# The end of an output projection: wo as the stationary operand, four columns on 128 partitions, and a store from contiguous partitions

## Chip, cores and metric

The kernel runs on one core of one Trainium2 chip. The metric is the device time of one execution in microseconds (us). Kernels that are compared were run in turn on the same chip. The profile's own span (first to last instruction) is usually about 1.8 us shorter than that time. The granted clock is the share of TensorE's full clock that the profile records. HBM is the memory that holds the caches and the result, SBUF the on-chip memory that the loads fill, PSUM the one in which products are summed.

## The reference, cut to what matters

```python
def reference(A_x, A_k_cache, A_v_cache, A_wq, A_wo, B_x, B_w1, B_b1, B_w2, B_b2):
    x = A_x                                    # 1 x 1 x 512
    xn = _layernorm(x, axis=-1)
    # 32 query heads, 8 key/value heads, 65536 keys, head size 128, then o (4096) @ wo (4096 x 512)
    return x + _A_ref(xn, A_k_cache, A_v_cache, A_wq, A_wo) + _B_ref(xn, B_w1, B_b1, B_w2, B_b2)
```

All tensors are bf16. One token attends to 65536 cached keys, so nearly all the work is reading the caches: 268 MB. The result is one row of 512 values, 1 KB.

## The kernel before

The kernel streams both caches, keeps the softmax statistics of each chunk, and combines them at the end. The last loads are the 4 MB of `wo`, in pieces: `wo0` (16 rows of 128 partitions), `wo1` (8 rows), `wo2` (4 rows), and for the last group of heads `wl0` (three heads) and `wl1` (one). What follows is the end, where the change lies. `oX_bf` holds the attention outputs of the first seven groups, `oT_all` those of the last, `f_rows` the sum of everything else as four fp32 rows on partitions 0, 32, 64 and 96 (other partitions are not selected by `row_sel`).

```python
    def fin_mm(kt, lhsT, rhs, reads, first, last, publish):
        sch.op(PE, lambda: pe.matmul(pR[32 * kt:32 * kt + 1, 0:128], lhsT=lhsT, rhs=rhs, start=first, stop=last),
               reads=reads, writes=[f"pss{R}"], publish=publish)

    R0 = WP[0][1] * HPG
    # ... wo0: 16 products of 512 columns into pss1, then f_rows = pss1 + f_rows on VectorE ...
    for i, (g0, n) in enumerate(WP):
        if i == 0:
            continue
        for r in range(g0 * HPG, (g0 + n) * HPG):
            for kt in range(KT):
                fin_mm(kt, oX_bf[:, r:r + 1], wo_sb[:, r, kt * 128:(kt + 1) * 128], ["oX", f"wo{i}"], r == R0, False,
                       r == (g0 + n) * HPG - 1 and kt == KT - 1)
    for kt in range(KT):
        fin_mm(kt, row_sel[:, :], f_rows[:, kt * 128:(kt + 1) * 128], ["f_rows", "row_sel"], False, False, kt == KT - 1)
    for h in range(HPG):
        for kt in range(KT):
            fin_mm(kt, oT_all[:, GE * HPG + h:GE * HPG + h + 1], wl_sb[:, h, kt * 128:(kt + 1) * 128],
                   ["oL", f"wl{0 if h < WH[0] else 1}"], False, h == HPG - 1, h == HPG - 1 and kt == KT - 1)
    NR = 32 * (KT - 1) + 1
    sch.op(DVE, lambda: dve.tensor_copy(out=fin_bf[0:NR, :], in_=pR[0:NR, 0:128]),
           reads=[f"pss{R}"], writes=["fin"])
    ev_out = sch.dma(
        SP,
        lambda: sp.dma_start(out=out[0, 0].rearrange("(kt p) -> kt p", p=128), in_=fin_bf[0:NR:32, :]),
        sem_out, reads=["fin"], writes=["out_dram"],
    )
    sch.wait_ev(SP, ev_out)
```

So the stationary operand (`lhsT`) is one column of attention output, `wo` streams past it 128 columns at a time, and the result is four rows of 128 values on four partitions. The whole kernel:

## Time and profile before

| | before |
|---|---|
| time, median of 6 runs | 658.36 us (658.16 to 658.62) |
| span of the profile | 656.4 us |
| read from HBM | 280.5 MB, 427 GB/s |
| granted TensorE clock, 652 to 653.5 us | 0.50 |
| start of the store's issue to the end of the span | 2.0 us |

Four lines of the page: the span, the busy tenths of the DMA engines in 40 slices, the traffic, and the shares of the chain that ended last.

```profile
span 656.4 us, 27873 instructions
...
DMA  9999999999999999999999999999999999999997
...
HBM read 280.50 MB, written 0.00 MB: 427 GB/s over the span
...
DMA 69%; PE 29%; issue 2%; SPq 0%; DVE 0%
...
```

The DMA engines are at nine tenths in all slices but the last, so the kernel runs at the speed of its loads until about 653 us. The tail after the last load is the only place where this change can cost or gain. The timeline of that tail has the columns start, duration, engine, line, operation, output<-inputs, sizes and count; in brackets stands how long the engine was idle before and what released it. PE is the product, PEld the load of its stationary operand.

```profile
...
start us, us, engine line op out<-in xcount [idle before <-releaser]
...
651.19 1.02 PE L808 MATMUL pss<-kv,oX_bf 128*1 128x128 bf16 x32 [0.21 <-DMA kv<-in_A_wo_dram]
...
652.48 0.59 PE L808 MATMUL pss<-kv,oX_bf 128*1 128x128 bf16 x16 [0.26 <-DMA kv<-in_A_wo_dram]
...
652.86 0.64 PE L808 MATMUL pss<-f_rows,row_sel 128*1 128x128 f32 x8
653.46 0.41 PEld L808 LDWEIGHTS pss<-kv,oT_all 128*1 128x1 bf16 x16 [0.47 <-DMA kv<-in_A_wo_dram]
653.46 0.55 PE L808 MATMUL pss<-kv,oT_all 128*1 128x128 bf16 x16
654.06 0.29 DVE L833 CAST fin_bf<-pss 97x128 bf16<-97x128 f32 x1 [2.33 <-PE pss L808]
654.38 0.63 SPq L837 DMA_DIRECT2D out_dram<-fin_bf  x1
```

Read it in steps. `wo1` lands and releases 32 products at 651.19; `wo2` releases 16 at 652.48. The four fp32 products of `f_rows` appear as eight passes from 652.86, and they end inside the wait for `wl`: the loads of the last 16 products are released by the transfer at 653.46. Those take 0.55 us, the VectorE copy 0.29 us, the issue of the store 0.63 us. After that the SyncE queue only waits for the store to land:

```profile
...
SPq L842 <- DMA out_dram<-fin_bf: 1.0, 1, 1.0
...
```

The windows of the same stretch, with busy us and count per engine, then the granted clock, the DMA share and GB/s:

```profile
...
core 0: us, PE busy (x) PEld busy (x) DVE busy (x) ACT busy (x) POOL busy (x), PEclk, DMA share, GB/s
...
652.40:653.50 1.10, 1.02 (x28) 0.56 (x32) 0.00 (x0) 0.00 (x0) 0.00 (x0) 0.50 0.32 110
653.50:655.50 2.00, 0.51 (x16) 0.25 (x16) 0.29 (x1) 0.00 (x0) 0.00 (x0) 0.97 0.00 0
...
```

### The profile page before, as it was taken

How to read it: one execution, taken by the hardware profiler on the slowest of the kernel's cores; microseconds unless marked ns; L12 is line 12 of the kernel's file. 1: busy time of each engine (PE TensorE's matmuls, PEld its weight loads, DVE VectorE, ACT ScalarE, POOL GpSimd, SP SyncE). 2: the span in 40 equal slices, each digit the busy share in tenths (PEclk: the TensorE clock that was granted, in tenths of full speed). 3: DMA queues.
4: the chain of work that ended last, by engine and by line, in shares of the span. 5: the costliest groups of instructions: out<-in, count | busy, mean ns of one | idle time of the engine just before them, and what ended most of it. 6: DMA issues, size and time to landing. Idle time of an engine off the chain costs nothing.

```text
span 656.4 us, 27873 instructions
## 1 busy us (share of the span) xinstructions
PE 536.7 (82%) x12634; PEld 507.4 (77%) x12634; DVE 276.3 (42%) x576; ACT 245.0 (37%) x454; POOL 2.9 (0%) x27
## 2 busy tenths in 40 slices
PE   2398699979789697878969788896978979797897
PEld 0187698969788696878959687895968879686886
DVE  3254162614435171452616245261633516153353
ACT  0144161613525162352605335161543516144251
POOL 0000000000000000000000000000000000000000
PEclk9688595967869596785959669595976959687695
DMA  9999999999999999999999999999999999999997
GB/s 369 431 445 417 438 423 439 435 427 459 403 439 439 421 445 423 435 431 433 445 415 447 415 447 421 427 461 401 457 413 453 423 423 435 427 459 406 433 429 302
DMA packets 8773, 280.64 MB, mean 428 GB/s; under 512 B 1082, under 2 KB 1596, under 8 KB 1724
## 3 DMA queue, kind: packets, MB, share of 16 engines
q1 hardware_dynamic: 8616, 280.50, 99.3%
q8 instruction: 7, 0.11, 0.1%
q10 hardware_dynamic: 148, 0.01, 0.0%
q14 instruction: 2, 0.02, 0.0%
HBM read 280.50 MB, written 0.00 MB: 427 GB/s over the span
## 4 chain that ended last, share of the span: by engine, by line
DMA 69%; PE 29%; issue 2%; SPq 0%; DVE 0%
DMA kv<-in_A_k_cache_dram 65%; PE pst L591 24%; DMA kv<-in_A_wo_dram 4%; PE pss L611 3%; PE pO L682 1%; PE pss L808 0%; PE pA L638 0%; PE pA L649 0%; SPq L479 0%; DVE pmax L619 0%; PE pA L698 0%; SPq L471 0%; SPq L468 0%; SPq L464 0%; DVE gmax L640 0%
## 5 line engine op out<-in xcount | busy, mean ns | idle before, releaser
L601 ACT ACTIVATE kt_ring<-pst 128x1024 bf16<-128x1024 bf16 x192 | 195.6, 1027 | 311.4 <-PE pst L591 310.0
L591 PE MATMUL pst<-ident_bf,kv 128*128 128x128 bf16 x4096 | 280.8, 234 | 34.8 <-DMA kv<-in_A_k_cache_dram 34.7
L591 PEld LDWEIGHTS pst<-ident_bf,kv 128*128 128x128 bf16 x4096 | 262.5, 106 | 43.2 <-DMA kv<-in_A_k_cache_dram 36.4
L599 DVE COPY kt_ring<-pst 128x1024 bf16<-128x1024 bf16 x320 | 210.6, 687 | 118.7 <-PE pst L591 116.6
L682 PE MATMUL pO<-P_bf,kv 128*128 128x4 bf16 x4096 | 115.1, 166 | 40.8 <-DMA kv<-in_A_v_cache_dram 34.9
L682 PEld LDWEIGHTS pO<-P_bf,kv 128*128 128x128 bf16 x4096 | 113.6, 104 | 42.2 <-DMA kv<-in_A_v_cache_dram 36.0
L611 PE MATMUL pss<-q_cur,kt_ring 128*128 128x4 bf16 x4096 | 111.9, 164 | 2.6 <-issue 2.6
L611 PEld LDWEIGHTS pss<-q_cur,kt_ring 128*128 128x128 bf16 x4096 | 109.3, 96 | 2.8 <-issue 2.8
L660 ACT ACTIVATE P_bf<-pss,negm 128x128 bf16<-128x128 f32 x128 | 50.9, 547 | 67.7 <-DVE negm L652 67.7
L691 DVE COPY o_all<-pO 128x4 f32 (+1 forms) x32 | 5.2, 162 | 124.0 <-PE pO L682 123.2
L619 DVE TENSOR_REDUCE pmax<-pss 128x4 f32<-128x512 f32 x32 | 22.1, 691 | 66.5 <-PE pss L611 66.5
L660 ACT ACTIVATION_READ_ACCUMULATOR P_bf<-pss,negm 128x1 f32 x128 | 35.3, 276 | 0.0
L649 PEld LDWEIGHTS pA<-diag,ones_f 4*128 4x128 f32 x64 | 12.6, 245 | 18.2 <-DVE diag L642 16.5
L638 PE MATMUL pA<-ident_f,pmax 128*4 128x128 f32 x64 | 14.3, 312 | 12.5 <-DVE pmax L619 12.5
L649 PE MATMUL pA<-diag,ones_f 4*128 4x4 f32 x64 | 15.4, 309 | 10.0 <-DVE diag L642 10.0
L638 PEld LDWEIGHTS pA<-ident_f,pmax 128*4 128x4 f32 x64 | 2.9, 84 | 15.7 <-DVE pmax L619 14.0
L640 DVE TENSOR_REDUCE gmax<-pA 4x1 f32<-4x128 f32 x32 | 8.8, 274 | 9.5 <-PE pA L638 9.5
L674 DVE COPY sums_all<-sums 128x8 f32 (+1 forms) x16 | 2.7, 172 | 23.4 <-ACT P_bf L660 23.4
L698 PE MATMUL pA<-sums_all,ones_f 128*128 128x128 f32 x32 | 12.4, 491 | 0.0
L652 DVE TENSOR_SCALAR negm<-pA 128x4 f32<-128x4 f32 x32 | 5.1, 160 | 10.8 <-PE pA L649 10.8
L698 PEld LDWEIGHTS pA<-sums_all,ones_f 128*128 128x128 f32 x32 | 8.1, 312 | 0.0
L642 DVE TENSOR_SCALAR diag<-ident_f,gmax 4x4 f32<-4x4 f32 x32 | 7.0, 217 | 1.1
(82 smaller groups left out, 49.4 us busy)
## 6 DMA issues: line engine op xcount, KB each, us to landing
kv<-in_A_k_cache_dram SPq DMA_DIRECT2D x32, 4096.0 KB, 27.7
kv<-in_A_v_cache_dram SPq DMA_DIRECT2D x4, 4096.0 KB, 24.7
kv<-in_A_wq_dram SPq DMA_DIRECT2D x1, 4096.0 KB, 12.2
kv<-in_B_w_dram SPq DMA_DIRECT2D x2, 1792.0 KB, 18.0
kv<-in_A_wo_dram SPq DMA_DIRECT2D x1, 2048.0 KB, 23.5
kv<-in_A_wo_dram SPq DMA_DIRECT2D x1, 1024.0 KB, 25.7
kv<-in_A_wo_dram SPq DMA_DIRECT2D x1, 512.0 KB, 26.5
kv<-in_A_wo_dram SPq DMA_DIRECT2D x1, 384.0 KB, 16.9
```

The costliest lines, as they stand in the source:

```text
L591: lambda tb=tb, at=at, b=b, tt=s * TPB + t: pe.transpose(pst[tb][:, at * 128:(at + 1) * 128], slot[b][:, tt, :], ident_bf[:, :]),
L599: e, fn = DVE, lambda tb=tb, dst=dst: dve.tensor_copy(out=dst, in_=pst[tb][:, :])
L601: e, fn = ACT, lambda tb=tb, dst=dst: act.activation(out=dst, in_=pst[tb][:, :], func=ACTF.Copy)
L611: lambda k=k, kb=kb, at=at, t=t: pe.matmul(pss[k][:, at:at + HPG], lhsT=kt_ring[:, kb * BCOL + t * 128:kb * BCOL + (t + 1) * 128], rhs=q_c ...
L619: lambda k=k: dve.tensor_reduce(out=pmax[:, :], in_=pss[k][:, 0:CW].rearrange("p (t j) -> p j t", j=HPG), axis=AX.X, op=ALU.max),
L638: sch.op(PE, lambda: pe.matmul(pA[0:HPG, PA_ST:PA_ST + 128], lhsT=pmax[:, 0:HPG], rhs=ident_f[:, :], start=True, stop=True), reads=["pmax" ...
L640: sch.op(DVE, lambda: dve.tensor_reduce(out=gmax4[:, :], in_=pA[0:HPG, PA_ST:PA_ST + 128], axis=AX.X, op=ALU.max), reads=["pA"], writes=[" ...
L642: sch.op(DVE, lambda: dve.tensor_scalar(out=diag4[:, :], in0=ident_f[0:HPG, 0:HPG], scalar1=gmax4[0:HPG, 0:1], scalar2=None, op0=ALU.mult) ...
L649: sch.op(PE, lambda: pe.matmul(pA[:, PA_SB:PA_SB + HPG], lhsT=ones_f[0:HPG, 0:128], rhs=diag4[0:HPG, 0:HPG], start=True, stop=True), reads ...
L660: lambda k=k, at=at, j=j, src=src: act.activation(out=P_v[k][:, :, j], in_=src[:, :, j], func=ACTF.Exp, bias=negm[:, at:at + 1], scale=1.0 ...
L682: lambda k=k, t=t: pe.matmul(pO[:, 0:HPG], lhsT=vslot[:, k * TPD + t, :], rhs=P_v[k][:, t, :], start=t == 0, stop=t == TPD - 1),
L698: sch.op(PE, lambda: pe.matmul(pA[:, PA_SUM:PA_SUM + NC], lhsT=ones_f[:, :], rhs=sums_all[:, :], start=True, stop=True), reads=["ones_f", ...
```

## The change

The idea is to turn the operands round. `wo` becomes the stationary operand (128 columns, taken at a step of four), the attention output streams one column, and the result stands as four columns on 128 partitions: partition p holds outputs 4p to 4p+3. The copy out of PSUM is then 128x4 in place of 97x128, and the store takes 8 contiguous bytes from each of 128 contiguous partitions in place of 256 bytes from each of four.

```diff
-    fin_bf = sb("fin_bf", [128, 128], BF)
+    fin_bf = sb("fin_bf", [128, KT], BF)
 ...
-        sch.op(PE, lambda: pe.matmul(pR[32 * kt:32 * kt + 1, 0:128], lhsT=lhsT, rhs=rhs, start=first, stop=last),
+        sch.op(PE, lambda: pe.matmul(pR[:, kt:kt + 1], lhsT=lhsT, rhs=rhs, start=first, stop=last),
 ...
-                fin_mm(kt, oX_bf[:, r:r + 1], wo_sb[:, r, kt * 128:(kt + 1) * 128], ["oX", f"wo{i}"], r == R0, False,
+                fin_mm(kt, wo_sb[:, r, kt:D:KT], oX_bf[:, r:r + 1], ["oX", f"wo{i}"], r == R0 and kt == 0, False,
 ...
-        fin_mm(kt, row_sel[:, :], f_rows[:, kt * 128:(kt + 1) * 128], ["f_rows", "row_sel"], False, False, kt == KT - 1)
+        fin_mm(kt, f_rows[:, kt:D:KT], row_sel[:, :], ["f_rows", "row_sel"], False, False, kt == KT - 1)
 ...
-            fin_mm(kt, oT_all[:, GE * HPG + h:GE * HPG + h + 1], wl_sb[:, h, kt * 128:(kt + 1) * 128],
+            fin_mm(kt, wl_sb[:, h, kt:D:KT], oT_all[:, GE * HPG + h:GE * HPG + h + 1],
 ...
-    sch.op(DVE, lambda: dve.tensor_copy(out=fin_bf[0:NR, :], in_=pR[0:NR, 0:128]),
+    sch.op(DVE, lambda: dve.tensor_copy(out=fin_bf[:, :], in_=pR[:, 0:KT]), reads=[f"pss{R}"], writes=["fin"])
 ...
-        lambda: sp.dma_start(out=out[0, 0].rearrange("(kt p) -> kt p", p=128), in_=fin_bf[0:NR:32, :]),
+        lambda: sp.dma_start(out=out[0, 0].rearrange("(p kt) -> p kt", kt=KT), in_=fin_bf[:, :]),
```

The code writes the products into the four columns as one accumulation group now: only the first of them has the start flag, and only the last the stop flag.

More of the change, by code (lines that the diff above doesn't have):

```diff
@@ L823, in bass_parallel_sum__gqa_block_cached__dense_activation_gelu__decode_kernel @@
             for kt in range(KT):
-                fin_mm(kt, oX_bf[:, r:r + 1], wo_sb[:, r, kt * 128:(kt + 1) * 128], ["oX", f"wo{i}"], r == R0, False,
+                fin_mm(kt, wo_sb[:, r, kt:D:KT], oX_bf[:, r:r + 1], ["oX", f"wo{i}"], r == R0 and kt == 0, False,
                        r == (g0 + n) * HPG - 1 and kt == KT - 1)
     for kt in range(KT):
-        fin_mm(kt, row_sel[:, :], f_rows[:, kt * 128:(kt + 1) * 128], ["f_rows", "row_sel"], False, False, kt == KT - 1)
+        fin_mm(kt, f_rows[:, kt:D:KT], row_sel[:, :], ["f_rows", "row_sel"], False, False, kt == KT - 1)
     for h in range(HPG):
         for kt in range(KT):
-            fin_mm(kt, oT_all[:, GE * HPG + h:GE * HPG + h + 1], wl_sb[:, h, kt * 128:(kt + 1) * 128],
-                   ["oL", f"wl{0 if h < WH[0] else 1}"], False, h == HPG - 1, h == HPG - 1 and kt == KT - 1)
-    NR = 32 * (KT - 1) + 1
-    sch.op(DVE, lambda: dve.tensor_copy(out=fin_bf[0:NR, :], in_=pR[0:NR, 0:128]),
-           reads=[f"pss{R}"], writes=["fin"])
+            fin_mm(kt, wl_sb[:, h, kt:D:KT], oT_all[:, GE * HPG + h:GE * HPG + h + 1],
+                   ["oL", f"wl{0 if h < WH[0] else 1}"], False, h == HPG - 1 and kt == KT - 1, h == HPG - 1 and kt == KT - 1)
+    sch.op(DVE, lambda: dve.tensor_copy(out=fin_bf[:, :], in_=pR[:, 0:KT]), reads=[f"pss{R}"], writes=["fin"])
     ev_out = sch.dma(
         SP,
-        lambda: sp.dma_start(out=out[0, 0].rearrange("(kt p) -> kt p", p=128), in_=fin_bf[0:NR:32, :]),
+        lambda: sp.dma_start(out=out[0, 0].rearrange("(p kt) -> p kt", kt=KT), in_=fin_bf[:, :]),
         sem_out, reads=["fin"], writes=["out_dram"],
```

## The prediction

Two terms in it: the PV product is that of the softmax weights with the value cache, and a pitch is the time from the start of one load to the start of the next.

> **What bounds the kernel.** The transfers. The page counts 280.5 MB read at 427 GB/s over a span of 656.4 us, the DMA row is at 9 tenths in 39 of 40 slices, and the chain of waits is 69% DMA. The change touches only the last 5 us. The timeline there: the three pieces of wo release PE at 651.19, 652.48 and 653.46 us; the last 16 matmuls take 0.55 us; the copy starts at 654.06; the store is issued at 654.38 for 0.63 us; its four 256 B packets move at 655.6 to 655.7, and the span ends at 656.4. The windows show a granted clock of 0.50 until about 653.5.
>
> **What changes.** 64 bf16 matmuls and 4 fp32 products (8 passes) in this tail stop loading one column (stationary) and streaming 128; they load 128 columns with a step of four elements and stream one. Weight loads now set the pace.
>
> - bf16 loads. At clock 0.50, the PV product (contiguous 128x128 loads, four columns) makes 128 pairs in 3.5 to 3.7 us, 28 ns a pair. The strided case is in the trace once: four loads of the normalised row with the same step of four, 0.21 us in all, 112 ns each, so a pitch of about 33 ns, against 25 ns for contiguous q rows at the same clock. [...] The old matmuls ran at about 24 ns each (16 in 0.55 us, latency taken off). So 32 + 16 + 16 products get about 10 ns slower each: 0.3, 0.15 and 0.15 us. The first two mostly hide in the waits for the next piece.
> - fp32 loads of f_rows. The h_rows loads (fp32, step two, clock 1.0) were 8 in 1.02 us, a pitch of 118 ns; at clock 0.50 I estimate 200 to 240 ns from the ones_f loads (232 to 334 ns each). Eight passes then take 1.0 (clock back at 1.0) to 1.9 us, in place of 0.64. Before, they fitted into the wait for the last piece of wo (0.47 us idle before 653.46). Now they start near 653.0 and end near 654.2 to 654.8, so the last 16 products start 0.7 to 1.3 us late.
> - Copy: 97x128 at 290 ns becomes 128x4, about 160 ns (as the 128x4 copies of o_all): -0.13 us.
> - Store: 128 pieces of 8 B on 16 engines instead of four of 256 B. The issue may be shorter (0.40 us for the 128-partition load of b1 against 0.63), small packets take 9 ns, eight per engine about 0.1 us. Estimate: 0 +/- 0.3 us.
>
> **Sum.** PE +0.8 to +1.5, copy -0.13, store about 0: +0.9 us, all on the critical path. Predicted 659.2 us, 8 in 10 between 657.8 and 660.9. Chances: faster by 2% 0.005, within 2% 0.99, slower 0.005.
>
> **What shows it.** fp32 passes of L808 at a pitch over 100 ns, with no wait for wo left before the last 16 products; bf16 loads with full 128x128 form at about 30 ns pitch; the copy near 0.16 us; issue to end of span about as before (2.0 us).
>
> **What would make it wrong.** [...] the clock returning earlier; 8 B writes to HBM landing late (slower) or many-engine stores landing sooner (faster); another chip.

Two passages are cut from it and marked: a sentence on which loads are fast, and a clause on strided loads among what would make it wrong. No term of the sum was in them, so the sum stands: PE +0.8 to +1.5, copy -0.13, store 0, together +0.9 us. Its bf16 term rests on the traced pitch of 33 ns and on 24 ns, worked out from 16 products in 0.55 us; its fp32 term rests on the traced 118 ns at clock 1.0 and, at 0.50, on the estimate of 200 to 240 ns from loads of 232 to 334 ns. That a load with a step of four keeps the 33 ns when it has 128 rows, not one, was not shown at that time; it was the author's estimate.

## The result, and the profile after

| | before | after |
|---|---|---|
| time, median of 6 runs | 658.36 us (658.16 to 658.62) | 660.95 us (660.72 to 661.21) |
| span of the profiled run | 656.4 us | 659.1 us |
| ratio of after to before | | 1.0039, 95% interval 1.0026 to 1.0052 |

A ratio here is the mean time of one kernel's fast runs over the mean of the other's fast runs of the same rounds, so it is not quite the ratio of the medians. The turned products are right: e3 and b2 below, which contain them, agree with the reference. The change costs 2.6 us, 0.4%: within 2%, but clear of the noise. The predicted 659.2 us had the direction, and about a third of the size: +0.8 us over 658.4 in place of +2.6. The measured median lies just above the upper end of the range, 660.9.

```profile
span 659.1 us, 27873 instructions
...
HBM read 280.50 MB, written 0.00 MB: 426 GB/s over the span
...
DMA 64%; PE 32%; issue 2%; DVE 0%; SPq 0%
...
```

The bytes are the same; DMA has a smaller share of the chain and PE a larger one. The tail, in the columns of before:

```profile
...
651.10 1.90 PEld L808 LDWEIGHTS pss<-oX_bf,kv 128*128 128x128 bf16 x48 [1.16 <-DMA kv<-in_A_wo_dram]
651.10 1.98 PE L808 MATMUL pss<-oX_bf,kv 128*128 128x1 bf16 x48 [0.23 <-DMA kv<-in_A_wo_dram]
652.91 1.95 PEld L808 LDWEIGHTS pss<-row_sel,f_rows 128*128 128x128 f32 x8
652.94 2.00 PE L808 MATMUL pss<-row_sel,f_rows 128*128 128x1 f32 x8
654.57 0.82 PEld L808 LDWEIGHTS pss<-oT_all,kv 128*128 128x128 bf16 x16
654.81 0.67 PE L808 MATMUL pss<-oT_all,kv 128*128 128x1 bf16 x16
655.51 0.16 DVE L832 CAST fin_bf<-pss 128x4 bf16<-128x4 f32 x1 [3.90 <-PE pss L808]
655.70 0.35 SPq L835 DMA_DIRECT2D out_dram<-fin_bf  x1
```

The start matches that of before to 0.1 us: `wo1` releases the products at 651.10. From there on PE is nearly never idle: a wait for `wo2` of about 0.1 us is left near 652.35 (windows of a tenth of a us show it), and none later. The 48 bf16 products run on to 652.9, and then eight fp32 loads of about 329 ns each (1.95 us for x8), one every 0.21 us ((654.57 - 652.91) / 8), push the last 16 products to 654.8. In the last lines no release by a transfer is left: the last traffic of the loads is in the quarter us from 653.00 (slices below), and the last 16 products start at 654.8. The copy starts at 655.51 in place of 654.06. The store is issued in 0.35 us in place of 0.63, but then the queue waits:

```profile
...
SPq L840 <- DMA out_dram<-fin_bf: 2.7, 1, 2.7
...
```

2.7 us in place of 1.0. The same two windows as before, for the clock of the stretch in which it was 0.97:

```profile
...
652.40:653.50 1.10, 1.10 (x19) 1.10 (x19) 0.00 (x0) 0.00 (x0) 0.00 (x0) 0.50 0.27 92
653.50:655.50 2.00, 1.97 (x23) 1.89 (x22) 0.00 (x0) 0.00 (x0) 0.00 (x0) 0.50 0.00 0
...
```

In 653.5 to 655.5 the clock is 0.50, with PE busy for 1.97 of the 2.00 us and PEld for 1.89; before it was 0.97, with PE busy for 0.51 and PEld for 0.25. And three windows at the very end show where the 2.7 us lie (the figure after the clock is the DMA share, then GB/s):

```profile
...
656.00:657.00 1.00, 0.00 (x0) 0.00 (x0) 0.00 (x0) 0.00 (x0) 0.00 (x0) 0.50 0.08 1
657.00:658.00 1.00, 0.00 (x0) 0.00 (x0) 0.00 (x0) 0.00 (x0) 0.00 (x0) 0.50 0.00 0
658.00:659.10 1.10, 0.00 (x0) 0.00 (x0) 0.00 (x0) 0.00 (x0) 0.00 (x0) 0.50 0.00 0
...
```

The store's packets show as a share of 0.08 between 656 and 657. After 657 the DMA engines move nothing, and still the span goes on to 659.1. The traffic of 650 to 660 us in 40 slices of a quarter us, before and then after, shows the movement of both stores as the lone 4 near the middle: at 655.50 to 655.75 before, 0.7 us before the end of that span, and at 656.50 to 656.75 after, 2.4 us before the end.

```profile
...
GB/s 410 332 365 426 336 381 225 201 221 201 176 160 66 0 0 0 0 0 0 0 0 0 4 0 0 0 0 0 0 0 0 0 0 0 0 0 0 0 0 0
...
GB/s 356 340 410 360 385 336 221 205 205 197 172 119 37 0 0 0 0 0 0 0 0 0 0 0 0 0 4 0 0 0 0 0 0 0 0 0 0 0 0 0
...
```

So what grew is neither issue nor, by more than about 0.1 us, movement, but the time between the last packet and the release of the wait. It is called the landing below.

The accounts of the two traces can be set side by side, in us from the same points: copy start 654.06 to 655.51 is +1.45; the copy 0.29 to 0.16 is -0.13; the issue 0.63 to 0.35 is -0.28; the wait 1.0 to 2.7 is +1.7. Together +2.7, the difference of the spans.

### The profile page after: what moved, and what is told of

The parts are those of the page before. It is cut to its first block, busy times and chain, and to the rows that moved or that the text cites. A ratio compares the mean times of both kernels' runs of the same rounds, so it can differ in the third digit from the quotient of the medians.

```text
span 659.1 us, 27873 instructions
## 1 busy us (share of the span) xinstructions
PE 540.2 (82%) x12634; PEld 512.2 (78%) x12634; DVE 276.3 (42%) x576; ACT 245.2 (37%) x454; POOL 2.9 (0%) x27
## 4 chain that ended last, share of the span: by engine, by line
DMA 64%; PE 32%; issue 2%; DVE 0%; SPq 0%
DMA kv<-in_A_k_cache_dram 60%; PE pst L591 26%; DMA kv<-in_A_wo_dram 4%; PE pss L611 4%; PE pO L682 2%; PE pss L808 0%; PE pA L638 0%; PE pA L649 0%; DVE pmax L619 0%; PE pA L698 0%; SPq L479 0%; DVE gmax L640 0%; DVE diag L642 0%; SPq L471 0%; SPq L468 0%
```

## The experiments

The theory after reading both traces: two costs that add, one on PE (the fp32 loads of `f_rows`) and one in the store (small pieces land late). The rivals: the store is late only because of when it is issued; all strided loads cost, not the fp32 ones; or the clock is to blame. Four kernels were run in the same rounds, five each, with the kernel before at 658.21 us (9 runs, 657.95 to 659.45). Their times scatter more than those of the first comparison, and mostly outside the span: one run of e1 took 660.92 us with a span of 657.8. The span of every run was recorded, and it is steadier, so both are given. The change itself was not run again in these rounds, so comparisons with it are across rounds, and are made by spans.

### e1_row_store: the change with the old store

```diff
-    sch.op(DVE, lambda: dve.tensor_copy(out=fin_bf[:, :], in_=pR[:, 0:KT]), ...)
+    sch.op(DVE, lambda: dve.tensor_copy(out=fin_bf[:, 0:KT], in_=pR[:, 0:KT]), ...)   # fin_bf is 128x128, zeroed at the start
-        lambda: sp.dma_start(out=out[0, 0].rearrange("(p kt) -> p kt", kt=KT), in_=fin_bf[:, :]),
+        lambda: sp.dma_start(out=out[0, 0].rearrange("(kt p) -> kt p", p=128), in_=fin_bf[0:97:32, :]),
```

> The changed kernel with the store of before put back: four 256 B rows from partitions 0, 32, 64 and 96 (wrong result on purpose, the sums stay on 128 partitions). Theory (two costs that add: PE +1.45 us, of which 1.65 us are the eight fp32 loads of f_rows; store +1.4 us, nearly all of it between the last packet and the last landing): 1.3 to 1.5 us faster than the changed kernel, so 659.5 to 659.9 against 658.4 before; the wait of the SyncE queue for the store falls from 2.7 to about 1.0 us. Rival (only PE costs, and the store lands late because it is issued at a later time or at a lower clock): no faster than the changed kernel, 660.7 to 661.1.

Measured: 660.17 us (659.60 to 660.92), ratio to before 1.0025 (1.0012 to 1.0039); spans 657.6 to 657.8, against 656.2 to 656.6 of before and 658.9 to 659.3 of the change. The result is wrong. The time is 0.3 us above the expected band with a wide scatter; the span has the expected size, 1.3 us below the change and 1.4 above before. The queue's wait for the store is back where it was, although PE, copy and the moment of issue (655.72) are those of the change:

```profile
...
SPq L841 <- DMA out_dram<-fin_bf: 1.0, 1, 1.0
...
```

So the late landing belongs to the form of the store, not to its moment or to the clock (0.50 from 655 to 656 here, where the store landed early; 1.00 in e2, where it landed late), and without it 1.4 us remain.

### e2_part_store: the kernel before with the new store

```diff
-        lambda: sp.dma_start(out=out[0, 0].rearrange("(kt p) -> kt p", p=128), in_=fin_bf[0:NR:32, :]),
+        lambda: sp.dma_start(out=out[0, 0].rearrange("(p kt) -> p kt", kt=KT), in_=fin_bf[:, 0:KT]),   # fin_bf zeroed at the start
```

> The kernel before with only the store of the change: 128 pieces of 8 B from 128 partitions (wrong result on purpose; PE and copy as before). Theory (two costs): 659.6 to 660.0, +1.3 to +1.5 us over before, the SyncE queue's wait for the store 2.7 us in place of 1.0 and its issue 0.35 in place of 0.63. Rival (only PE costs): within 0.3 us of before.

Measured: 659.55 us (659.12 to 660.31), ratio 1.0016 (1.0003 to 1.0030); spans 657.3 to 657.6, +0.9 to +1.2 us over the 656.4 of before. Wrong result. The rival (only PE costs) falls; the size is a little below the one expected, since the wait was 2.3 us in this run, not 2.7:

```profile
...
SPq L843 <- DMA out_dram<-fin_bf: 2.3, 1, 2.3
...
```

By medians the spans of e1 (+1.4) and e2 (+1.1) add up to +2.5 us over before, against the +2.65 of the change. The 0.15 left over is within the spread of this wait, which is not steady from run to run (below).

### e3_bf16_rows: the change with `f_rows` as a bf16 operand

```diff
+    f_rows_bf = sb("f_rows_bf", [128, D], BF)
-    row_sel = sb("row_sel", [128, 1], F32)
+    row_sel = sb("row_sel", [128, 1], BF)
-    sch.op(DVX, lambda: dve.tensor_tensor(out=f_rows[:, :], in0=pss[1][:, :], in1=f_rows[:, :], op=ALU.add),
+    sch.op(DVX, lambda: dve.tensor_tensor(out=f_rows_bf[:, :], in0=pss[1][:, :], in1=f_rows[:, :], op=ALU.add),
-        fin_mm(kt, f_rows[:, kt:D:KT], row_sel[:, :], ["f_rows", "row_sel"], ...)
+        fin_mm(kt, f_rows_bf[:, kt:D:KT], row_sel[:, :], ["f_rows_bf", "row_sel"], ...)
```

> The changed kernel with the sum of f_rows written in bf16, and a bf16 selector, so that its four products are four bf16 loads in place of eight fp32 loads; the store stays as changed. Theory (fp32 loads are the PE cost, 207 ns each at the 0.50 clock, bf16 loads with a step of four 38 ns each): the fp32 part 1.65 us becomes about 0.15, the last 16 products wait for the last piece of wo again and start near 653.45, the copy starts near 654.2 in place of 655.5: 1.2 to 1.4 us faster than the changed kernel, 659.6 to 659.9. Rival (it is the strided loads of all 64 products that cost, fp32 no more than the rest): at most 0.3 us faster, 660.6 to 661.0.

Measured: 659.28 us (659.22 to 659.74), ratio to before 1.0016 (1.0003 to 1.0030); spans 657.4 to 657.9. The result is right. That is 1.7 us below the change's median, though of other rounds; by spans it is 1.5 us (657.5 against 659.05, medians), a little more than the 1.2 to 1.4 expected. In the two profiles the copy starts 1.11 us earlier than in the change, and the other 0.5 us is the wait for the store, which was 2.2 us in this run in place of 2.7. The timeline shows the wait for `wl` back:

```profile
...
653.18 0.22 PEld L809 LDWEIGHTS pss<-row_sel,f_rows_bf 128*128 128x128 bf16 x4
...
653.67 0.61 PEld L809 LDWEIGHTS pss<-oT_all,kv 128*128 128x128 bf16 x16 [0.28 <-DMA kv<-in_A_wo_dram]
...
654.40 0.16 DVE L833 CAST fin_bf<-pss 128x4 bf16<-128x4 f32 x1 [2.79 <-PE pss L809]
...
```

Four bf16 loads take 0.22 us where eight fp32 ones took 1.95, and the last 16 products are again released by the transfer. They are strided like all others. The rival that the step of four makes PE late falls.

### e4_both: bf16 `f_rows` and the old store

The edits of e1 and e3 together.

> Both edits together (bf16 f_rows and the store of four rows; wrong result on purpose). Theory (two costs that add, nothing else): 658.1 to 658.6, within 0.3 us of before, since the copy is 0.13 us shorter and the last 16 products take about 0.1 us more. Rival (something else in the change costs, such as the clock or the bf16 products): 0.5 us or more above before.

Measured: 658.10 us (658.04 to 658.54), ratio 0.9998 (0.9984 to 1.0011); spans 656.2 to 656.8. Wrong result. With both suspects taken out, the copy starts when it did before (654.06), and the store lands after the same wait:

```profile
...
654.07 0.16 DVE L834 CAST fin_bf<-pss 128x4 bf16<-128x4 f32 x1 [2.72 <-PE pss L810]
...
SPq L842 <- DMA out_dram<-fin_bf: 1.0, 1, 1.0
...
```

The spans have medians of 656.3 and 656.4 us; the interval of the ratio alone would leave room for about 1 us. There is no third cost of a size that these runs can see. The clock was 0.50 to the end in this kernel too (its windows show 0.50 after 654), so the clock alone is not the cost either. It may still have made the fp32 loads dearer: a pass has a pitch of 118 ns in the `h_rows` loads at clock 1.0 and of about 210 ns at 0.50. No run had these loads at the end at clock 1.0.

### b2_loads: what a load costs

The changed kernel, with three rounds of loads after its copy, each with a one-column product:

```diff
+    for rd in range(3):
+        # 16 x lhsT=wo_sb[:, n, 0:128]                  bf16, step 1   (L848)
+        # 16 x lhsT=wo_sb[:, n, 1:D:4]                  bf16, step 4   (L850)
+        #  4 x lhsT=f_rows[:, n * 128:(n + 1) * 128]    fp32, step 1   (L852, 8 passes)
+        #  4 x lhsT=f_rows[:, ...:2]                    fp32, step 2   (L854, 8 passes)
+        #  4 x lhsT=f_rows[:, n:D:4]                    fp32, step 4   (L856, 8 passes)
```

> The changed kernel, right result, then three rounds of loads with one-column products on PE: 16 bf16 with step one, 16 bf16 with step four, 4 fp32 products (8 passes) with step one, two and four. Theory (fp32 alone makes it slow, the step does not): fp32 passes at about 207 ns each at clock 0.50 and near 118 ns at 1.0 for each step; bf16 at 28 to 38 ns with either step. Rival (the step makes it slow): step-one loads clearly faster than step-four ones of the same type, fp32 with step one under 130 ns at clock 0.50, bf16 with step one under 30 and with step four over 36.

Measured, one look (right result). The first round in the timeline:

```profile
...
655.72 0.50 PEld L848 LDWEIGHTS pss<-oT_all,kv 128*128 128x128 bf16 x16 [0.34 <-DVE fin_bf L832]
...
656.14 0.61 PEld L850 LDWEIGHTS pss<-oT_all,kv 128*128 128x128 bf16 x16
...
656.67 1.79 PEld L852 LDWEIGHTS pss<-row_sel,f_rows 128*128 128x128 f32 x8
...
658.34 1.83 PEld L854 LDWEIGHTS pss<-row_sel,f_rows 128*128 128x128 f32 x8
...
660.05 1.97 PEld L856 LDWEIGHTS pss<-row_sel,f_rows 128*128 128x128 f32 x8
...
661.73 0.71 PEld L848 LDWEIGHTS pss<-oT_all,kv 128*128 128x128 bf16 x16
...
```

Taking the starts of the PEld lines: bf16 with step one (656.14 - 655.72) / 16 = 26 ns a load, with step four (656.67 - 656.14) / 16 = 33 ns; fp32 with step one (658.34 - 656.67) / 8 = 209 ns, step two 214 ns, step four (661.73 - 660.05) / 8 = 210 ns. The step costs 7 ns of a bf16 load and, to within 5 ns, nothing of an fp32 one. (The 0.71 us at 661.73 holds a wait behind the fp32 loads; by the starts of the PE products, the later rounds give 27 and 33 ns.) The 26 ns is just under the 28 to 38 expected for bf16 and within the rival's figure for step one (under 30); the rival's other figures (step four over 36 ns, fp32 with step one under 130 ns) did not come. The type costs: an fp32 product is two passes of about 210 ns, 420 ns against 33. The part of the expectation that was for clock 1.0 could not be read, for the clock never rose. The last window of the third round, after 15 us of this:

```profile
...
671.00:674.00 3.00, 3.00 (x15) 3.00 (x15) 0.00 (x0) 0.00 (x0) 0.00 (x0) 0.50 0.00 0
...
```

PE and PEld are busy for all of it, at 0.50. The pitch of 118 ns of the `h_rows` loads, which the prediction used as its lower bound, was measured at clock 1.0; at 0.50 the figure is about 210.

All loads of b2 are 128x128; fewer columns were not tried.

### b1_stores and b3_stores: which stores land late

Both are the kernel before (right result) with 14 more stores of one tile to a scratch tensor, each waited for. Each was run once, b1 on the chip of e1 to e4 and b3 on another one. One store stands for all here; the forms are in the table below.

```diff
+    scr = nc.dram_tensor("scr", [65536], BF, kind="Internal").ap()
+    def store(fn):
+        sch.wait_ev(SP, sch.dma(SP, fn, sem_out, reads=["st"], writes=["scr"]))
+    store(lambda: sp.dma_start(out=scr[0:512].rearrange("(p n) -> p n", n=4), in_=st_bf[:, 0:4]))   # 128 x 8 B, packed
```

> The kernel before, right result, then 14 stores one after the other, each waited for, to a scratch tensor: 4x256 B (twice), 128x8 B packed, 128x8 B at steps of 64 B and of 512 B, 16x64 B, 32x32 B, 64x16 B, 16x8 B, 4x8 B, 128x64 B, 128x256 B, and the first two forms again. The figure to read is the time from issue to landing. Theory A (small pieces that share a stretch of HBM are written one after the other): packed 128x8 B lands about 1.7 us later after its issue than 4x256 B, the form at 512 B steps as soon as the 4x256 B form (within 0.3 us), 16x64 B likewise. Theory B (the number of small pieces costs, wherever they lie): all three 128x8 B forms are alike, 64x16 B and 32x32 B lie between in proportion, and 128x64 B is slow as well. Theory C (sixteen engines in place of four cost): 16x8 B and 16x64 B are as slow as 128x8 B.

The queue's waits in b1, longest first. A wait is listed at the line of the instruction after it, so the wait at L851 is for the store of L850. L850 and L860 store 128 x 8 B packed, L851 the same 64 B apart, L849 4 x 256 B.

```profile
...
SPq L861 <- DMA scr<-st_bf: 2.5, 1, 2.5
SPq L851 <- DMA scr<-st_bf: 2.3, 1, 2.3
...
SPq L852 <- DMA scr<-st_bf: 1.1, 1, 1.1
SPq L850 <- DMA scr<-st_bf: 1.1, 1, 1.1
...
```

> The kernel before, right result, then 14 stores to scratch, each waited for: 4x256 B, 128x8 B packed, then at steps of 16, 32 and 64 B, 64x8 B, 32x8 B and 16x8 B packed, 128x16 B packed, 128x32 B packed, 64x8 B at steps of 64 B, 128x8 B at steps of 16 B and packed again, 4x256 B again. Figures: the queue's wait after each issue; 1.0 to 1.1 us is the plain case, 2.3 to 2.5 the packed 128x8 B. Theory A1 (pieces that share a 32 B stretch are slow): steps of 32 B plain, steps of 16 B slow (1.5 us or more), 128x16 B slow like steps of 16 B, 128x32 B plain; 64x8 B about half the excess of 128x8 B, 32x8 B a quarter. Theory A2 (pieces that share a 64 B stretch are slow): as A1, but steps of 32 B and 128x32 B also clearly over 1.3 us. Theory A3 (all pieces of one whole KB take turns): the excess falls smoothly with the step, 16 B about half, 32 B about a quarter, and 64x8 B has half the excess or all of it.

And in b3, where L849 and L860 store 128 x 8 B packed, L850 and L851 the same 16 and 32 B apart, L854 32 x 8 B packed, and L856 128 x 16 B packed (each wait again one line further on):

```profile
...
SPq L855 <- DMA scr<-st_bf: 4.3, 1, 4.3
SPq L861 <- DMA scr<-st_bf: 2.9, 1, 2.9
SPq L850 <- DMA scr<-st_bf: 2.8, 1, 2.8
...
SPq L857 <- DMA scr<-st_bf: 2.0, 1, 2.0
...
SPq L851 <- DMA scr<-st_bf: 1.5, 1, 1.5
...
SPq L852 <- DMA scr<-st_bf: 1.1, 1, 1.1
...
```

The two together, in us of waiting after the issue:

| store | b1 | b3 |
|---|---|---|
| 4 x 256 B | 1.0, 1.1, 1.0 | 1.0, 1.0 |
| 128 x 8 B, packed | 2.3, 2.5 | 2.8, 2.9 |
| 128 x 8 B, 16 B apart | | 1.5, 1.1 |
| 128 x 8 B, 32 B apart | | 1.1 |
| 128 x 8 B, 64 B apart | 1.1 | 1.1 |
| 128 x 8 B, 512 B apart | 1.1 | |
| 64 x 8 B, packed | | 2.7 |
| 32 x 8 B, packed | | 4.3 |
| 16 x 8 B, packed | 1.0 | 1.8 |
| 4 x 8 B, packed | 1.0 | |
| 64 x 8 B, 64 B apart | | 1.2 |
| 64 x 16 B, packed | 1.2 | |
| 128 x 16 B, packed | | 2.0 |
| 32 x 32 B and 16 x 64 B, packed | 1.0, 1.0 | |
| 128 x 32 B, packed | | 1.1 |
| 128 x 64 B and 128 x 256 B, packed | 1.1, 1.1 | |

What follows from it. 128 pieces of 8 B are not slow in themselves: at 32, 64 or 512 B apart they land as soon as four rows of 256 B (1.1 us against 1.0 to 1.1). Nor is it slow to write from many partitions in place of four (16 x 64 B in 1.0 us, 128 x 256 B in 1.1). That removes theories B and C of b1 and leaves A. Every form whose pieces do not share a stretch of 32 B was plain, 1.0 to 1.2 us. Every wait over 1.2 us is of a form in which two or more pieces share such a stretch: that is A1 of b3, as far as the 32 B go (steps of 16 B took 1.5 and 1.1 us, steps of 32 B 1.1). A2 falls with the steps of 32 B and with 128 x 32 B (1.1 us each), A3 with the steps of 32 B.

A1 was wrong on the size. It expected half the excess for 64 pieces and a quarter for 32; they waited 2.7 and 4.3 us, and the same form twice took 1.0 and 1.8 (on two chips), or 1.5 and 1.1 (in one run, where A1 had expected 1.5 or more). 4 x 8 B packed and 64 x 16 B packed share too and took 1.0 and 1.2. So in these runs no store without sharing landed late, but sharing alone is not enough, and how late is neither proportional to the number of pieces nor steady.

The trace files also hold a landing event for each DMA engine of a store (no view of the profile prints them; they were read from the files). Counted from the store's last packet, the four of before came after 0.27 to 0.34 us, and the sixteen of e5 below, with spaced pieces, after 0.21 to 0.37. Those of the change came after 0.20 to 1.99 us: the first as early as elsewhere, the rest strung out. In the packed 32 x 8 B of b3 most of the late ones follow each other at steps of about 0.4 us, up to 3.69. So in these two packed stores the landings of the engines followed one another, which is what theory A supposed. Why they do is not shown by these runs and stays open.

### e5_spaced_store: small pieces, spaced, in the kernel itself

```diff
 # on top of e3
-        lambda: sp.dma_start(out=out[0, 0].rearrange("(p kt) -> p kt", kt=KT), in_=fin_bf[:, :]),
+        lambda: sp.dma_start(out=scr[0:4096].rearrange("(p n) -> p n", n=32)[:, 0:KT], in_=fin_bf[:, :]),
 # and zeros are stored to out at the start
```

> The changed kernel with bf16 f_rows and the same 128 pieces of 8 B, but written 64 B apart into a scratch tensor; the output itself gets zeros at the start (wrong result on purpose). Theory (8 B pieces are not slow in themselves, only packed into one short stretch of HBM): like the kernel with both edits, or a little faster as the issue is 0.3 us shorter: 657.8 to 658.4, 0.9 to 1.4 us faster than with the packed store (659.3), and the SyncE queue's wait for it about 1.1 us in place of 2.2. Rival (in the kernel, just after the stream of loads, small pieces land late wherever they lie): no faster than 659.0, wait over 2 us.

Measured on another chip, with before at 658.21 us (658.09 to 659.87): 658.00 us (657.87 to 658.38), ratio 0.9994 (0.9980 to 1.0007); spans 656.1 to 656.5. Wrong result. The same 128 pieces of 8 B from the same partitions, 64 B apart, cost nothing that the runs can see. That they went to a scratch tensor is not the reason, for the same pieces packed in the scratch tensor of b1 and b3 waited 2.3 to 2.9 us, and these 1.1:

```profile
...
SPq L847 <- DMA scr<-fin_bf: 1.1, 1, 1.1
...
```

The rival, that the stream of loads before it makes small pieces late, falls.

No version beat both kernels. The output is contiguous, so spaced pieces are not to be had, and e3, the best right one with the change, is slower than before. e4 and e5 mark what the idea could give at best: the time of before, within the noise of about 0.2%, because the last products cannot start before `wl` lands (653.3 to 653.7 in these profiles) in either form.

## Why the prediction was wrong

The direction, the place and the first cost were right; the range was missed because one term of the sum, the store, was given as zero. Of the 1.8 us between the predicted +0.9 and the +2.7 of the two profiles, 1.4 is that term; most of the rest is PE near the top of its range.

- **What bounds the kernel, and that only the tail matters: right.** The lines up to 651.1 us agree to 0.1 us, and e4 is back at the time of before.
- **bf16 loads: right.** "About 33 ns" was measured as 33 ns in b2 and as 38 ns over the 48 products of the change (1.90 us, less one load of 0.12, over 47 steps; this holds the short wait for `wo2`). The step of four cost 7 ns a load in b2, 33 against 26.
- **fp32 loads: right that they push back the last products, size at the upper edge.** The prediction gave "1.0 (clock back at 1.0) to 1.9 us" and a start of the last products 0.7 to 1.3 us late. The clock did not come back, the passes took 1.66 us from the first load to the load of the last products, and the copy started 1.45 us late. PE was given as +0.8 to +1.5, so this held, near the top.
- **Copy: right.** -0.13 us, to 0.16.
- **Store: wrong, and this is the step that failed.** "Estimate: 0 +/- 0.3 us", "issue to end of span about as before (2.0 us)". The issue did get shorter (0.35 against 0.63) and the packets are short (9 ns each for 8 B in the trace file), both as written. But the prediction costed issue and movement from the trace and left the landing as it was. The wait took 2.7 us in place of 1.0. Over both traces the store's term is +1.4 us (1.7 of wait less 0.28 of issue); by e2, alone, it is +0.9 to +1.2 in spans. The prediction named it among what would make it wrong ("8 B writes to HBM landing late") without giving it room in the range.

The sum with the terms as measured in the traces: +1.45 - 0.13 - 0.28 + 1.7 = +2.7. The loads on which the store's term was built (`b1`, 28 B a partition) write to SBUF, not to HBM, and no store of small pieces was in the trace of before. The trace of after shows where the cost of this store lay: no movement after 657 us, the last landing 1.99 us after the last packet, and the end at 659.1. In the trace of before only the landing of four 256 B pieces could be read (0.27 to 0.34 us after the last packet). So the landing of small pieces was the one part of this term that no trace had shown, and the uncertainty belonged there.

## What to carry to other kernels

The tail after the last load was a sum of latencies here (+1.45 - 0.13 - 0.28 + 1.7 us), so cost each link to its end: for a store that is issue (0.35 or 0.63 us in the two traces), movement (0.1 to 0.2 us) and landing (most of the 1.7 us). In these runs the landing went with how the bytes lay in HBM. Give each piece a stretch of at least 32 B of its own where the layout allows it; here 128 packed pieces of 8 B waited 1.2 to 1.9 us longer than four rows of 256 B, and the same pieces 32 B apart (one store) or 64 B apart (three stores) waited no longer. Before an operand becomes stationary look at its type: a cheap streaming fp32 operand (eight passes in 0.64 us) became two loads of 0.21 us a product (1.95 us for the eight), and bf16 removed nearly all of it (0.22 us for four loads).
